# Sixteen tiles of x in a transformer block: for the second eight, 32x32 block turns on VectorE in place of TensorE transposes

## The chip, the cores and the metric

One core of one Trainium2 chip runs the kernel. Its engines are TensorE (PE in the profile), VectorE (DVE), ScalarE (ACT), GpSimd (POOL) and SyncE (SP), which issues most of the DMA transfers. Each engine takes its instructions from a queue of its own, in the order in which they were written, and they meet through semaphores. The metric is the device time of one execution in microseconds, as the median of three runs.

## The reference, cut to what matters

The block works on 2048 rows of 1024 columns in float32.

```
h   = x + attention(layernorm(x))
out = h + relu(layernorm(h) @ w1) @ w2

attention(x): q, k, v = x @ wqkv                 32 heads of 32
              phi_q, phi_k = softmax(+-(q @ w_phi)), softmax(+-(k @ w_phi))
              o = phi_q (phi_k^T v) / (phi_q sum(phi_k) + 1e-6)
              return o @ wo
layernorm(x): (x - mean) / sqrt(var + 1e-5)      per row
```

The layernorm of the first line is the one that the change touches: its output, turned so that the columns of x lie on the partitions, is the stationary operand of the products with the weights of q, k and v.

## The kernel before, in words

The 2048 rows are 16 tiles of 128, in two halves of 8. A float32 product is made of two parts of each operand, a high one (the value rounded to TensorE's fp32r type) and a low one (the value minus the high part), and three matmuls: high by high (L182), high by low of the weight (L183), low by high (L184). So the second of the three needs the weight's low part, and the third needs the low part of x. One such triple is a step, and eight steps (the eight 128-column blocks of x) are an item: one tile by one 128x512 piece of the weights, for each of the 8 blocks k. The first half runs 32 kv items (4 pieces s of the key and value weights by 8 tiles) and 16 q items (2 pieces by 8), and then the second half the same. In steps, the piece of the weights changes at 0, 64, 128, 192 (kv), 256, 320 (q) for the first half and 384, 448, 512, 576 (kv), 640, 704 (q) for the second. This text calls such a place a switch. After these 96 items come the product with wo and the MLP, which the change leaves alone.

Everything beside the matmuls is written into the stream by hand: `when(step, f)` puts the work f behind the matmuls of that step, and so sets its place in the queue of every engine that it uses. What the steps of this text refer to:

- **Weight units** (class Units, L69 to L137). A unit is one 128x512 block of weights: loaded raw, copied to its high part by ACT (L125), and subtracted to its low part by POOL or DVE (L129; in kv pieces the even k go to POOL and the odd ones to DVE). The ring has 10 places and a piece takes 8, so at a switch most units of the next piece are made while PE works on the last item of the old one, each as a place comes free.
- **Layernorm of x** (L211 to L253). A load, the statistics on DVE (`ln_stats`, L222), three instructions on POOL for the scale and shift (`ln_power`, L231 to L233, called the trio here), the normalization on ACT (`ln_norm`, L239), eight PE transposes into two PSUM banks (`ln_turn`, L246), and out of each bank a high part by ACT (L178) and a low part by DVE (L179), into the tile xT.
- **The second half's tiles** (t = 8 to 15). Their statistics and trio are made early, at steps 98+16i and 102+16i (i = t-8). The normalization and the turn come late, around the q items of the last q piece of the first half (steps 320 to 384), where xT of tile t-8 comes free. For that x is loaded a second time.
- **POOL's other work in the same stretch.** `t_sum` (L363) makes sums of blocks of the MLP's weights, in place in a 512 KB tile: a load, four subtractions on POOL, a store (t<-b), with two such tiles, so that a load waits until the store before the last is done. `kv_z` (L452, L454) adds up the key features (zacc). L544 copies small sums of the q items (smq).
- **Places on SP**: SP issues raw loads, t_sum's loads and stores, and the loads of x in program order, and waits in its queue for what each needs.

Of the kernel before, what the change touches and what calls it, by code (L numbers as in the profile page):

```python
# [9 lines left out]
F32 = mybir.dt.float32  # L10
F32R = mybir.dt.float32r
AF = mybir.ActivationFunctionType
ALU = mybir.AluOpType
AX = mybir.AxisListType

P = 128
S = 2048
D = 1024
# [3 lines left out]
NT = S // P  # L22
HT = NT // 2
NK = D // P
# [116 lines left out]
def kernel(  # L141
# [12 lines left out]
    v, act, pool, pe, sp = nc.vector, nc.scalar, nc.gpsimd, nc.tensor, nc.sync  # L154
# [4 lines left out]
    lnp = ctx.enter_context(tc.tile_pool(name="lnp", bufs=2))  # L159
    dram = ctx.enter_context(tc.tile_pool(name="scratch", bufs=1, space=bass.MemoryType.DRAM))  # L160
# [12 lines left out]
    def f32(ap):  # L173
        return ap.bitcast(F32)
# [14 lines left out]
    def do(n, k, f, *args):  # L189
        at[n, k].append((f, args))  # L190
# [6 lines left out]
    ed = [dram.tile([8, 2, P, 512], F32, name=f"ed{b}") for b in range(4)]  # L197
    smd = [dram.tile([2, P, P], F32, name=f"smd{b}") for b in range(4)]
    hd = [dram.tile([P, D], F32, name=f"hd{t}") for t in range(NT)]

# [6 lines left out]
    xin, xst, xnt = {}, {}, {}  # L209

    def ln_load(key, parts):  # L211
        xin[key] = xlp.tile([P, D], F32, name="xl") if key[0] == "x" and key[1] >= HT and key[1] % 4 > 1 else \
            lnp.tile([P, D], F32, name="xin")
        n = D // len(parts)
        for j, p in enumerate(parts):
            sp.dma_start(xin[key][:, j * n:(j + 1) * n], p)
# [10 lines left out]
    def ln_power(key):  # L227

        mv = xst[key]
        sc = scx[:, key[1] - HT, 0, :] if key[0] in "sf" else lnp.tile([P, 2], F32, name="sc", bufs=4)  # L230
        pool.tensor_scalar_add(sc[:, 0:1], mv[:, 1:2], LN_EPS)  # L231
        pool.tensor_tensor(out=sc[:, 0:1], in0=sc[:, 0:1], in1=half, op=ALU.pow)
        pool.tensor_scalar(sc[:, 1:2], mv[:, 0:1], sc[:, 0:1], -1.0, op0=ALU.mult, op1=ALU.mult)  # L233
        xst[key] = sc

    def ln_norm(key):
        sc, src = xst.pop(("s", key[1]) if key[0] == "x" and key[1] >= HT else key), xin.pop(key)
        xnt[key] = src if key[0] == "h" else fp_ln.tile([P, D], F32, name="xn")
        act.activation(xnt[key], src, AF.Identity, bias=sc[:, 1:2], scale=sc[:, 0:1])  # L239

    def ln_turn(key, j, dst=None):
# [10 lines left out]
        if j == 1:  # L252
            del xnt[key]  # L253


    right = ExitStack()
    xpool = right.enter_context(tc.tile_pool(name="xT", bufs=HT, side="right"))
# [2 lines left out]
    fp_ln = kps.enter_context(tc.tile_pool(name="xn", bufs=2, side="right"))  # L260
# [159 lines left out]
    xT = {}  # L420
# [298 lines left out]
    def ln_pair(i, stage):  # L719

        keys = [("h", 4 * r + i) for r in range(2)]
        if stage == 0:
            for key in keys:
                ln_load(key, [hd[key[1]]])
# [222 lines left out]
    def item(gen, *args, keys):  # L947
        items.append((gen, args + (keys,)))
        steps.extend((k,) for k in keys)
        return len(items) - 1  # L950
# [11 lines left out]
    for b, tiles in enumerate(groups):  # L962
        for hf in range(2):

            pairs = b == 0 and hf == 0
            for j in range(0, 4, 2 if pairs else 1):
# [3 lines left out]
                for half in range(2):  # L970
                    n = item(wo_pair, tiles[j:j + 2], hf, half, keys=[("wo", hf, 4 * half + k // 2) for k in range(8)])
# [18 lines left out]
    def x_part(t):  # L990
        return [x[t * P:(t + 1) * P, :]]
# [6 lines left out]
    def when(step, f, *args):  # L998

        if step < 8 * first_up:  # L1000
            do(step // 8, step % 8, f, *args)
        else:
            do(first_up + (step - 8 * first_up) // 4, step % 4, f, *args)
# [4 lines left out]
    for t in range(1, NT):  # L1008
        n = t - 1 if t < HT else q_n[1, t - HT] + 1
        turn = 8 * n + 1  # L1010
        if t < HT:
            stages = X_STEPS.get(t, (turn - 22, turn - 12, turn - 9, turn - 6, turn, turn + 3))
        else:

            early = 80 + 16 * (t - HT)
            when(early, ln_load, ("s", t), x_part(t))
            when(early + 18, ln_stats, ("s", t))
            when(early + 18, xin.pop, ("s", t))
            when(early + 22, ln_power, ("s", t))
            load_ = turn - 88 + 8 * (t - HT) if t < HT + 4 else turn - 36  # L1020
            stages = (load_, None, None, turn - 8, turn + 1, turn + 1)
        for step, f, *args in zip(stages, (ln_load, ln_stats, ln_power, ln_norm), [("x", t)] * 4):
            if step is not None:
                when(step, f, *args, *([x_part(t)] if f is ln_load else []))
        do(n, 0, x_open, t)
        for j in range(2):
            when(stages[4 + j], ln_turn, ("x", t), j, lambda t=t: xT[t])
# [146 lines left out]
    def up_step(b, p, m):  # L1174

        return up0 + 4 * (up_n[b, p, m] + 1 - first_up)

    for j, m in enumerate(UP):

        for g in range(2):  # L1180
            step = up0 + (8 * j + (-62, -29)[g] if j < 4 else 6 * (j - 4) + 4 + 2 * g)
# [4 lines left out]
            step = up_step(0, NP - 1, m) + 2 * j  # L1186
# [16 lines left out]
    for n, (w, p, j) in enumerate((w, p, j) for w in (1, 2) for p in range(NP) for j in range(2)):  # L1203
        step = sums_at[n]
# [7 lines left out]
    for b in range(2):  # L1212
        for m in DOWN:
            n = down_n[b, m, NP - 1] + 1
            name, more = {1: "x1", 5: "x4", 6: "x2", 4: "x3"}.get(m), \
# [15 lines left out]
    scx = consts.tile([P, HT, 4, 2], F32, name="scx")  # L1231
# [18 lines left out]
    ln_stats(("x", 0))  # L1250
    ln_power(("x", 0))
    ln_norm(("x", 0))
    x_open(0)
    ln_load(("x", 2), x_part(2))
# [70 lines left out]
```

## Time and profile before

| | |
|---|---|
| median of 3 runs | 1872.97 us (1872.37 to 1873.45) |
| the profiled execution, its own time | 1870.48 us |
| its span | 1868.7 us |
| PE busy | 1856.5 us, 99% of the span |
| DVE busy | 1063.8 us, 57% |
| POOL busy | 979.0 us, 52% |
| ACT busy | 770.5 us, 41% |
| TensorE clock granted | nine tenths or more in each of 40 slices |
| HBM read, written | 293.21 MB, 137.89 MB |

A row of the timeline has the start in us, the length, the engine, the line of the kernel, the operation with its output and inputs, and in brackets the engine's idle time before it with what ended it. Rows that stand together are a group: xcount is the number of instructions, and the length runs to the end of the last. A matmul's length is that from its entry to its modelled end, and matmuls overlap, so the distance between two starts is the price of one. In the table of groups each row has busy time in all and the mean of one in ns. A row of waits has the total, the number of times and the longest. The names are those of the kernel; L numbers are the lines of the kernel before.

### The profile page before, as it was taken

The numbers are of one execution on the slowest core, as the hardware profiler recorded it, in microseconds if no ns is written. First come the engines' busy times: TensorE is split into PE (matmuls) and PEld (weight loads), VectorE is DVE, ScalarE is ACT, GpSimd is POOL, SyncE is SP. The second block draws the span as 40 slices with busy tenths as digits, with TensorE's granted clock in tenths as the row PEclk, the third lists the DMA queues.
The fourth block names the chain that finished last, engine by engine and source line by source line (L and its number), as shares of the span: only waits on it lengthen the run. The fifth ranks groups of instructions, "written<-read, shape, count | busy, mean of one in ns | idle before, by whom it ended". The sixth has DMA issues, their size and how long they took to land.

```text
span 1868.7 us, 28840 instructions
## 1 busy us (share of the span) xinstructions
PE 1856.5 (99%) x10064; PEld 1516.3 (81%) x10064; DVE 1063.8 (57%) x1655; ACT 770.5 (41%) x1379; POOL 979.0 (52%) x991
## 2 busy tenths in 40 slices
PE   9999999999999999999999999999999999999999
PEld 7777788888887777888888888888888888888887
DVE  7787678677689878575555653443433333343333
ACT  5322245233333333354455554444444444444442
POOL 4887745888947988343333222222344444444443
PEclk9999999999999999999999999999999999999999
DMA  7988798666575676887888975666677677777765
GB/s 229 286 294 288 231 289 270 190 203 202 178 227 181 223 243 203 280 278 232 247 262 259 324 249 184 193 201 205 225 223 215 216 218 239 238 215 217 216 216 177
DMA packets 333635, 433.04 MB, mean 232 GB/s; under 512 B 28720, under 2 KB 194608, under 8 KB 333488
## 3 DMA queue, kind: packets, MB, share of 16 engines
q1 hardware_dynamic: 299696, 414.41, 70.1%
q10 hardware_dynamic: 33792, 16.78, 3.2%
q8 instruction: 79, 1.29, 0.3%
q14 instruction: 68, 0.56, 0.1%
HBM read 293.21 MB, written 137.89 MB: 231 GB/s over the span
## 4 chain that ended last, share of the span: by engine, by line
PE 93%; DVE 3%; POOL 1%; issue 1%; ACT 0%; DMA 0%; SPq 0%; ACTq 0%; DVEq 0%; POOLq 0%
PE mm L182 24%; PE mm L183 24%; PE mm L184 24%; PE ac L182 4%; PE ac L184 4%; PE ac L183 4%; PE tp L184 2%; PE tp L183 2%; PE tp L182 2%; PE tp L246 1%; PE ac L465 1%; PE ac L650 1%; DVE qsm L534 0%; DVE qe L637 0%; POOL w L129 0%
## 5 line engine op out<-in xcount | busy, mean ns | idle before, releaser
L129 POOL TENSOR_TENSOR w<-raw,w 128x512 fp32r<-128x512 f32 x353 | 469.0, 1331 | 698.3 <-ACT w L125 663.2
L125 ACT ACTIVATE w<-raw 128x512 fp32r<-128x512 f32 x686 | 409.4, 626 | 508.8 <-PE mm L184 232.4
L129 DVE TENSOR_TENSOR w<-raw,w 128x512 fp32r<-128x512 f32 x333 | 271.0, 815 | 511.6 <-ACT w L125 507.6
L182 PE MATMUL mm<-w,xT 128*128 128x512 f32 x768 | 306.0, 398 | 0.0
L183 PE MATMUL mm<-w,xT 128*128 128x512 f32 x768 | 300.2, 391 | 0.4 <-POOL w L401 0.4
L184 PE MATMUL mm<-w,xT 128*128 128x512 f32 x768 | 299.6, 390 | 0.0
L182 PE MATMUL mm<-hT,w 128*128 128x512 f32 x672 | 261.5, 389 | 0.0
L183 PE MATMUL mm<-hT,w 128*128 128x512 f32 x672 | 261.5, 389 | 0.0
L184 PE MATMUL mm<-hT,w 128*128 128x512 f32 x672 | 261.5, 389 | 0.0
L182 PEld LDWEIGHTS mm<-w,xT 128*128 128x128 f32 x768 | 144.4, 188 | 35.2 <-issue 4.1
L184 PEld LDWEIGHTS mm<-w,xT 128*128 128x128 f32 x768 | 144.4, 188 | 30.9
L363 POOL TENSOR_TENSOR b<-b 128x256 f32<-128x256 f32 x176 | 143.6, 816 | 48.0 <-DMA b<-in_w_dram 38.6
L183 PEld LDWEIGHTS mm<-w,xT 128*128 128x128 f32 x768 | 144.6, 188 | 29.2 <-POOL w L401 1.0
L184 PE MATMUL mm<-w 128*128 128x512 f32 x392 | 152.6, 389 | 0.0
L182 PE MATMUL mm<-w 128*128 128x512 f32 x392 | 152.6, 389 | 0.0
L183 PE MATMUL mm<-w 128*128 128x512 f32 x392 | 152.6, 389 | 0.0
L182 PEld LDWEIGHTS mm<-hT,w 128*128 128x128 f32 x672 | 126.2, 188 | 26.4
L183 PEld LDWEIGHTS mm<-hT,w 128*128 128x128 f32 x672 | 126.2, 188 | 26.2
L184 PEld LDWEIGHTS mm<-hT,w 128*128 128x128 f32 x672 | 126.2, 188 | 26.0
L183 PEld LDWEIGHTS mm<-w 128*128 128x128 f32 x392 | 73.6, 188 | 15.3
L184 PEld LDWEIGHTS mm<-w 128*128 128x128 f32 x392 | 73.6, 188 | 15.2
L182 PEld LDWEIGHTS mm<-w 128*128 128x128 f32 x392 | 73.6, 188 | 15.3
(173 smaller groups left out, 3106.0 us busy)
## 6 DMA issues: line engine op xcount, KB each, us to landing
raw<-t SPq DMA_DIRECT2D x224, 256.0 KB, 3.9
raw<-ad SPq DMA_DIRECT2D x196, 256.0 KB, 3.0
raw<-in_w_dram SPq DMA_DIRECT2D x168, 256.0 KB, 3.1
ad<-c SPq DMA_DIRECT2D x112, 256.0 KB, 3.6
b<-in_w_dram SPq DMA_DIRECT2D x44, 512.0 KB, 5.8
t<-b SPq DMA_DIRECT2D x44, 512.0 KB, 5.0
ad<-s SPq DMA_DIRECT2D x84, 256.0 KB, 4.1
ed<-qe ACTq DMA_DIRECT2D x64, 256.0 KB, 4.1
```

The costliest lines, as they stand in the source:

```text
L125: nc.scalar.activation(w[:, 0, :], raw[1], AF.Copy)
L129: eng.tensor_tensor(out=w[:, 1, :], in0=raw[1], in1=w[:, 0, :].bitcast(F32), op=ALU.subtract)
L182: pe.matmul(ps, a_hi, b_hi, start=first, stop=False, skip_group_check=more)
L183: pe.matmul(ps, a_hi, b_lo, start=False, stop=False, skip_group_check=more)
L184: pe.matmul(ps, a_lo, b_hi, start=False, stop=last, skip_group_check=more)
L246: pe.transpose(pt[:, k, :], xn[:, (4 * j + k) * P:(4 * j + k + 1) * P], ident)
L363: pool.tensor_tensor(out=tsum[*u, *out], in0=tsum[*u, *a], in1=tsum[*u, *b], op=ALU.subtract)
L465: pe.matmul(kv_ps[s][g][32 * i:32 * (i + 1), 0:64], vt[:, 32 * h:32 * (h + 1)], phi[:, 64 * h:64 * (h + 1)], start=first, stop=last)
L650: pe.matmul(banks[g][32 * c:32 * (c + 1), 256 * j:256 * (j + 1)], kvL[rows, 2 * q + h // 4, 32 * (h % 4):32 * (h % 4 + 1)], phT_of[u - 1 + ...
```

## The change

For the tiles 8 to 15 the late second load, the normalization there, the 64 PE transposes and the reads of PSUM go. In their place:

- **Early**, at steps counted from early = 80+26i: the load at +0, the statistics at +12, the trio at +16, the normalization on ACT at +20 (`far_norm`), which writes the normalized tile into a second buffer with its 32-column blocks exchanged (runs of 128 bytes), and at +23 a store by SP (`far_keep`, 512 KB in pieces of 1 KB) to a DRAM tile xm whose rows and blocks lie so that 32x32 block turns finish the transpose.
- **Late**, at steps counted from late_ = 330+11i: at -30 SP loads the tile back (`far_back`, 512 KB), at +0 DVE turns it in place by 32x32 blocks (`far_turn`, one instruction 128x1024), at +4 ACT makes the high part (`far_high`) and at +7 POOL the low part (`far_low`), one instruction 128x1024 each. Both read the turned tile with an innermost step of 1 KB and write xT in order.

So the low parts of these eight tiles move from DVE (two instructions 128x512 from PSUM) to POOL (one of 128x1024 from SBUF), and the trio moves from steps 102+16i to 96+26i.

```diff
--- before.py
+++ after.py
@@ -197,6 +197,7 @@
     ed = [dram.tile([8, 2, P, 512], F32, name=f"ed{b}") for b in range(4)]
     smd = [dram.tile([2, P, P], F32, name=f"smd{b}") for b in range(4)]
     hd = [dram.tile([P, D], F32, name=f"hd{t}") for t in range(NT)]
+    xm = {t: dram.tile([P, D], F32, name=f"xm{t}") for t in range(HT, NT)}
 
 
 
@@ -209,8 +210,7 @@
     xin, xst, xnt = {}, {}, {}
 
     def ln_load(key, parts):
-        xin[key] = xlp.tile([P, D], F32, name="xl") if key[0] == "x" and key[1] >= HT and key[1] % 4 > 1 else \
-            lnp.tile([P, D], F32, name="xin")
+        xin[key] = lnp.tile([P, D], F32, name="xin")
         n = D // len(parts)
         for j, p in enumerate(parts):
             sp.dma_start(xin[key][:, j * n:(j + 1) * n], p)
@@ -227,14 +227,14 @@
     def ln_power(key):
 
         mv = xst[key]
-        sc = scx[:, key[1] - HT, 0, :] if key[0] in "sf" else lnp.tile([P, 2], F32, name="sc", bufs=4)
+        sc = scx[:, key[1] - HT, 0, :] if key[0] == "f" else lnp.tile([P, 2], F32, name="sc", bufs=4)
         pool.tensor_scalar_add(sc[:, 0:1], mv[:, 1:2], LN_EPS)
         pool.tensor_tensor(out=sc[:, 0:1], in0=sc[:, 0:1], in1=half, op=ALU.pow)
         pool.tensor_scalar(sc[:, 1:2], mv[:, 0:1], sc[:, 0:1], -1.0, op0=ALU.mult, op1=ALU.mult)
         xst[key] = sc
 
     def ln_norm(key):
-        sc, src = xst.pop(("s", key[1]) if key[0] == "x" and key[1] >= HT else key), xin.pop(key)
+        sc, src = xst.pop(key), xin.pop(key)
         xnt[key] = src if key[0] == "h" else fp_ln.tile([P, D], F32, name="xn")
         act.activation(xnt[key], src, AF.Identity, bias=sc[:, 1:2], scale=sc[:, 0:1])
 
@@ -252,6 +252,33 @@
         if j == 1:
             del xnt[key]
 
+
+    def far_norm(t):
+        sc, src = xst.pop(("s", t)), xin.pop(("s", t))
+        xin["m", t] = y = lnp.tile([P, D], F32, name="xin")
+        act.activation(y.rearrange("p (a c k) -> p c a k", a=4, c=NK), src.rearrange("p (c a k) -> p c a k", a=4, c=NK),
+                       AF.Identity, bias=sc[:, 1:2], scale=sc[:, 0:1])
+
+    def far_keep(t):
+        sp.dma_start(xm[t].rearrange("(a t) (g x) -> (t g) a x", a=4, g=4),
+                     xin.pop(("m", t)).rearrange("p (a x) -> p a x", a=4))
+
+    def far_back(t):
+        xnt["x", t] = y = xlp.tile([P, D], F32, name="xl") if t % 4 > 1 else fp_ln.tile([P, D], F32, name="xn")
+        sp.dma_start(y, xm[t])
+
+    def far_turn(t):
+        v.transpose(xnt["x", t], xnt["x", t])
+
+    def far_view(y):
+        return y.rearrange("p (g c t) -> p c t g", g=4, c=NK)
+
+    def far_high(t):
+        act.activation(xT[t][:, 0].rearrange("p c (t g) -> p c t g", g=4), far_view(xnt["x", t]), AF.Copy)
+
+    def far_low(t):
+        lo, hi = (xT[t][:, s].rearrange("p c (t g) -> p c t g", g=4) for s in (1, 0))
+        pool.tensor_tensor(out=lo, in0=far_view(xnt.pop(("x", t))), in1=f32(hi), op=ALU.subtract)
 
     right = ExitStack()
     xpool = right.enter_context(tc.tile_pool(name="xT", bufs=HT, side="right"))
@@ -1012,13 +1039,17 @@
             stages = X_STEPS.get(t, (turn - 22, turn - 12, turn - 9, turn - 6, turn, turn + 3))
         else:
 
-            early = 80 + 16 * (t - HT)
+            early, late_ = 80 + 26 * (t - HT), 330 + 11 * (t - HT)
             when(early, ln_load, ("s", t), x_part(t))
-            when(early + 18, ln_stats, ("s", t))
-            when(early + 18, xin.pop, ("s", t))
-            when(early + 22, ln_power, ("s", t))
-            load_ = turn - 88 + 8 * (t - HT) if t < HT + 4 else turn - 36
-            stages = (load_, None, None, turn - 8, turn + 1, turn + 1)
+            when(early + 12, ln_stats, ("s", t))
+            when(early + 16, ln_power, ("s", t))
+            when(early + 20, far_norm, t)
+            when(early + 23, far_keep, t)
+            when(late_ - 30, far_back, t)
+            do(n, 0, x_open, t)
+            for step, f in ((0, far_turn), (4, far_high), (7, far_low)):
+                when(late_ + step, f, t)
+            continue
         for step, f, *args in zip(stages, (ln_load, ln_stats, ln_power, ln_norm), [("x", t)] * 4):
             if step is not None:
                 when(step, f, *args, *([x_part(t)] if f is ln_load else []))
```

On PE the only difference in order is that the eight rows of L246 between triples of the second half's tiles are gone. On POOL two places matter. The first is the switch of step 128: `w<-raw,w` are low parts of the weight units for that switch, `b<-b` is t_sum, and the trio is L231 to L233. Before:

```order
L231 TENSOR_SCALAR scx<-mv 128x1
L232 TENSOR_TENSOR scx<-scx,half 128x1
L233 TENSOR_SCALAR scx<-mv,scx 128x1
L363 TENSOR_TENSOR b<-b 128x256 x2
L129 TENSOR_TENSOR w<-raw,w 128x512
L363 TENSOR_TENSOR b<-b 128x256
L454 TENSOR_TENSOR zacc_361<-zacc_361,kphi 128x512
L363 TENSOR_TENSOR b<-b 128x256
L129 TENSOR_TENSOR w<-raw,w 128x512 x2
```

The kernel with the change, the same place:

```order
L390 TENSOR_TENSOR b<-b 128x256 x2
L129 TENSOR_TENSOR w<-raw,w 128x512
L390 TENSOR_TENSOR b<-b 128x256
L231 TENSOR_SCALAR sc<-mv 128x1
L232 TENSOR_TENSOR sc<-sc,half 128x1
L233 TENSOR_SCALAR sc<-mv,sc 128x1
L481 TENSOR_TENSOR zacc_369<-zacc_369,kphi 128x512
L390 TENSOR_TENSOR b<-b 128x256
L129 TENSOR_TENSOR w<-raw,w 128x512 x2
```

The trio that stood ahead of the batch now stands in it, in front of the addition to zacc and of the last two weight units. The second place on POOL is the stretch from the switch of step 384 (its last unit opens the rows) towards that of step 448. Before:

```order
L129 TENSOR_TENSOR w<-raw,w 128x512
L363 TENSOR_TENSOR b<-b 128x256
L544 TENSOR_TENSOR smq<-qsm 128x16 x2
L363 TENSOR_TENSOR b<-b 128x256 x3
L454 TENSOR_TENSOR zacc_360<-zacc_360,kphi 128x512
L544 TENSOR_TENSOR smq<-qsm 128x16 x2
L363 TENSOR_TENSOR b<-b 128x256 x4
L454 TENSOR_TENSOR zacc_360<-zacc_360,kphi 128x512
L363 TENSOR_TENSOR xn<-xn 128x256 x4
L454 TENSOR_TENSOR zacc_360<-zacc_360,kphi 128x512
L363 TENSOR_TENSOR xn<-xn 128x256 x4
```

With the change, where L281 is `far_low`, L390 is t_sum, L481 is kv_z and L571 is the copy of small sums:

```order
L129 TENSOR_TENSOR w<-raw,w 128x512
L281 TENSOR_TENSOR xT<-xn,xT 128x1024
L390 TENSOR_TENSOR b<-b 128x256
L571 TENSOR_TENSOR smq<-qsm 128x16 x2
L390 TENSOR_TENSOR b<-b 128x256 x3
L481 TENSOR_TENSOR zacc_368<-zacc_368,kphi 128x512
L281 TENSOR_TENSOR xT<-xl,xT 128x1024
L571 TENSOR_TENSOR smq<-qsm 128x16 x2
L390 TENSOR_TENSOR b<-b 128x256 x4
L481 TENSOR_TENSOR zacc_368<-zacc_368,kphi 128x512
L390 TENSOR_TENSOR xn<-xn 128x256 x2
L281 TENSOR_TENSOR xT<-xl,xT 128x1024
```

Three instructions of 128x1024 now stand among the same work, the low parts of tiles 13, 14 and 15; that of tile 12 stands just ahead of these rows, before two copies of small sums. The four subtractions of one t_sum tile (xn) now stand on both sides of the last low part.

## The prediction

> **What bounds the kernel now.** I read the head of the profile first, then PE's waits, then the timelines of PE and POOL around the switches. From the head, and the first rows of PE's waits:
>
> ```profile
> span 1868.7 us, 28840 instructions
> PE 1856.5 (99%) x10064; PEld 1516.3 (81%) x10064; DVE 1063.8 (57%) x1655; ACT 770.5 (41%) x1379; POOL 979.0 (52%) x991
> ```
>
> ```profile
> PE ac L650 <- DVE qe L637: 2.8, 2, 2.4
> PE tp L246 <- ACT xn L239: 2.2, 1, 2.2
> PE tp L1244 <- POOL ones L1240: 1.6, 1, 1.6
> PE mm L183 <- POOL wf L129: 1.5, 1, 1.5
> PE mm L183 <- POOL w L401: 0.4, 1, 0.4
> ```
>
> PE bounds it: 1856.5 of 1868.7 us, and its waits sum to 8.5 us. None is longer than 2.4 us. So the change can gain only what leaves PE's queue, and loses whatever new wait it puts in front of a matmul. The other engines are half idle on average, which says nothing of the places where PE is close behind them.
>
> **What it removes from PE.** The timeline of PE around the turn of one tile of the second half:
>
> ```profile
> 268.10 0.39 PE L184 MATMUL mm<-w,xT 128*128 128x512 f32 x1
> ...
> 268.78 0.39 PE L184 MATMUL mm<-w,xT 128*128 128x512 f32 x1
> 269.01 1.03 PE L246 MATMUL tp<-ident,xn 128*128 128x128 f32 x8
> ...
> 270.35 0.39 PE L184 MATMUL mm<-w,xT 128*128 128x512 f32 x1
> ```
>
> From one L184 to the next a step takes 268.78 - 268.10 = 0.68 us; with the eight transposes between, 270.35 - 268.78 = 1.57. A tile's transposes cost 0.89 us of PE, though the row says 1.03 (overlap). Eight tiles: 8 x 0.89 = 7.15 us. They start behind a matmul, without idle time, so all of it is gained if nothing else is late. PE then reaches the switch of step 384 seven tiles, 6.26 us, earlier, and all later work 7.15 us earlier.
>
> **What it puts on the other engines.** The nearest groups:
>
> ```profile
> L239 ACT ACTIVATE xn<-xin,scx 128x1024 f32<-128x1024 f32 x4 | 5.0, 1241 | 4.5 <-DMA xl<-in_x_dram 2.1 <-DMA raw<-in_wv_dram 1.4 <-ACT qe L525 1.0
> L178 ACT ACTIVATE xT<-tp 128x512 fp32r<-128x512 f32 x32 | 17.9, 595 | 20.5 <-PE tp L246 20.4
> L179 DVE TENSOR_TENSOR xT<-tp,xT 128x512 fp32r<-128x512 f32 x32 | 20.7, 679 | 11.1 <-ACT xT L178 11.1
> L637 DVE STREAM_TRANSPOSE qe<-qe 128x1024 f32<-128x1024 f32 x32 | 39.3, 1227 | 7.5 <-POOL qe L631 5.6 <-POOL qe L626 1.8
> L781 DVE STREAM_TRANSPOSE y<-xin 128x1024 f32<-128x1024 f32 x4 | 8.2, 2040 | 1.2 <-ACT xin L796 1.2
> L579 POOL TENSOR_TENSOR xl<-xl,zb 128x1024 f32<-128x1024 f32 x6 | 14.4, 2401 | 0.0
> t<-b SPq DMA_DIRECT2D x44, 512.0 KB, 5.0
> ```
>
> - DVE, per tile: one in-place turn, 1.23 us by L637, for two subtractions of 0.68. That is neutral, -0.13 us.
> - ACT, per tile: the normalization stays (1.24 us by L239), and one copy of 128x1024 takes the place of two of 0.60. Bounds for the copy: 1.2 (no price for the strided read) to 2.0 (1.2 x 2040/1227, the ratio of L781, which writes in 16-byte steps, to L637, which doesn't). I take 1.6: +0.4 us on an engine 41% busy. I cost it at nothing: the moved normalizations stand ahead of no weight unit that they could delay by more than their own 1.24 us, and ACT has idle time before each unit.
> - SP and DMA: eight loads of 512 KB go and eight come; eight stores of 512 KB are new. The like of them, t<-b, lands in 5.0 us; the steps between store and reading back are over 100 for every tile, and 30 steps (30 x 0.68 = 20 us) lie between load and turn. A store waits in SP's queue for ACT's normalization, and raw loads stand behind it; they are issued some 20 us before use. Cost nothing, bounds -1 to +2 us.
> - POOL: +8 low parts of 128x1024, and the trios moved. This is what decides.
>
> **The trios, early.** The timeline of POOL around the switch of step 128, and PE's use of the last unit but one that POOL makes there:
>
> ```profile
> 109.41 0.22 POOL L231 TENSOR_SCALAR scx<-mv 128x1 f32<-128x1 f32 x1 [2.91 <-DVE mv L224]
> ...
> 110.38 0.70 POOL L233 TENSOR_SCALAR scx<-mv,scx 128x1 f32<-128x1 f32 x1
> ...
> 115.34 1.77 POOL L454 TENSOR_TENSOR zacc<-zacc,kphi 128x512 f32<-128x512 f32 x1
> 117.08 1.18 POOL L363 TENSOR_TENSOR b<-b 128x256 f32<-128x256 f32 x1
> 118.22 3.00 POOL L129 TENSOR_TENSOR w<-raw,w 128x512 fp32r<-128x512 f32 x2
> ```
>
> ```profile
> 120.75 0.39 PE L183 MATMUL mm<-w,xT 128*128 128x512 f32 x1
> ```
>
> The trio takes 109.41 to 111.08, 1.67 us, in a gap of POOL. With the change it stands ahead of the row of 115.34, behind which POOL has no gap until the two units are done, the first at 118.22 + 1.50 = 119.72. PE takes that one at 120.75, so there is 1.03 us of room; 1.67 - 1.03 = 0.64 is the most it can be late. I take 0.5. The trio of tile 14 (step 252) stands in the same way inside the batch for step 256; I give it 0.3, between nothing and 0.64. The other six fall between switches. Sum 0.8 us, bounds 0 and 1.3.
>
> **The low parts, late.** POOL, and PE's first use of a POOL unit after the switch of step 384:
>
> ```profile
> 275.35 3.19 POOL L363 TENSOR_TENSOR b<-b 128x256 f32<-128x256 f32 x4 [5.12 <-DMA b<-in_w_dram]
> 282.12 3.20 POOL L363 TENSOR_TENSOR b<-b 128x256 f32<-128x256 f32 x4 [3.23 <-DMA b<-in_w_dram]
> 289.08 2.39 POOL L363 TENSOR_TENSOR b<-b 128x256 f32<-128x256 f32 x3 [3.41 <-DMA b<-in_w_dram]
> 296.14 0.74 POOL L363 TENSOR_TENSOR b<-b 128x256 f32<-128x256 f32 x1 [3.62 <-DMA b<-in_w_dram]
> 302.76 3.19 POOL L363 TENSOR_TENSOR b<-b 128x256 f32<-128x256 f32 x4 [2.85 <-DMA b<-in_w_dram]
> 306.71 1.28 POOL L129 TENSOR_TENSOR w<-raw,w 128x512 fp32r<-128x512 f32 x1 [0.77 <-ACT w L125]
> ```
>
> ```profile
> 312.99 0.39 PE L183 MATMUL mm<-w,xT 128*128 128x512 f32 x1
> ```
>
> Before step 384 POOL runs at the pace of t_sum's transfers, a sum every 6.9 us whatever PE does, and its last sum ends at 302.76 + 3.19 = 305.95. PE, 6.26 us earlier, wants the first unit at 312.99 - 6.26 = 306.73; POOL can have it at 305.95 + 1.28 = 307.23 at best. That is 0.5 us late, and I take 0.8 for the queue behind it (bounds 0 and 1.5). This is a wait that the gain itself makes. The low parts of tiles 8 to 11 fall into the gaps of 3.23, 3.41, 3.62 and 2.85 us behind the sums: up to about 3.2 us each they are hidden but for 0.4 in the last, and above that the sums slip.
>
> The low parts of tiles 12 to 15 fall into the stretch behind it. One row of the table of busy time by stretch for all of 312.7 to 348, and the first unit of the next switch, step 448:
>
> ```profile
> 312.70:348.00 35.30, 35.30 (x204) 29.05 (x204) 25.72 (x52) 8.65 (x16) 27.05 (x35) 1.00 0.85 255
> ```
>
> ```profile
> 353.12 1.30 POOL L129 TENSOR_TENSOR w<-raw,w 128x512 fp32r<-128x512 f32 x1 [5.12 <-ACT w L125]
> ```
>
> POOL is busy for 27.05 us of it (the last column of busy times). With the change that work starts at about 310.2 (307.2, and 3 us for the two units and the copies ahead), so it ends at 310.2 + 27.05 + 4L = 337.25 + 4L, where L is the price of one low part. It must be over when ACT hands over the first unit of step 448: 353.12 - 7.15 + 0.8 = 346.8, and 0.8 us of room behind that (as at the other switches, where it was 1.03 above), 347.6. At L = 2.4 the end is 346.85, no wait; above, each 0.1 us of L costs 0.4 us.
>
> **The price L.** No row shows a GpSimd subtraction that reads with a 1 KB step. Low end: 2.40 us, L579, two streams of 128x1024. High end: 2.40 x 2040/1227 = 4.0, the whole instruction dearer by the ratio that strided access costs a DVE turn. Only one of its two input streams is strided, so I take half of 2.40 as dearer by that ratio: 2.40 + 1.20 x 0.66 = 3.2.
>
> [...]
>
> **The sum.** With L = 3.2: 7.15 - 0.8 (trios) - 0.8 (step 384) - 0.4 (last gap) - 2.8 (337.25 + 12.8 - 347.6 = 2.45, and 0.35 for POOL's waits among it) = 2.35 us. Against the profiled execution's 1870.48 that gives 1868.1; its time stood 2.5 us under the median of 1872.97, and the forecast for the median is 1872.97 - 2.35 = 1870.6, say 1870.7. By the price of both bounds the gain lies between 7.15 - 1.6 = 5.5 (L = 2.4) and about -3.3 (L = 4.0: sums slip by 4 x 0.72 = 2.9, the stretch costs 6.0).
>
> **The rivals.**
> - Strided reads cost POOL nothing: L = 2.4, all low parts hidden, gain 5.5, 1867.5. For it: GpSimd's contiguous rows (2.40 us for 1024 columns) are far slower than a DVE row, so the access may not be its limit. Against: L781.
> - The other side: POOL becomes the bound around the switches of steps 384 and 448, since the whole instruction pays. It decides from the L at which the gain is eaten: 7.15 - 1.6 - (4 x (L - 3.28)) - (4 x (L - 2.4) - 0.4) = 0 at L = 3.6. At 4.0, and 0.3 more for subtractions of DVE beside it, L = 4.3: 4 x 1.02 + 7.2 = 11.3 against 5.55, slower by 5.7, 1878.7.
> - L = 3.6, midway between 3.2 and 4.0, as if one stream and part of the other paid: the gain is just eaten, 1873. [...]
> - All eight moved trios stand in PE's way, not two: 8 x 0.64 = 5.1 in place of 0.8, 1870.7 + 4.3 = 1875. Against: six stand between switches, where POOL's units have microseconds to spare.
> - The change doesn't do what it says, the transposes' time returning as idle time before other matmuls: excluded up to the waits named, since PE waits so little today.
>
> **How the numbers follow.** Chances: L near 3.2 0.33 (its own range 1868.5 to 1873), L near 2.4 0.25, L near 3.6 0.12, L from 4.0 0.23, all trios 0.07. The time forecast is that of the first. No measurement of this kernel tells less than about 0.2%, 3.75 us, from no change. Faster by more, below 1869.2, takes L under 2.9: all of the second case and a sixth of the first, 0.30. Slower by more, above 1876.7, takes L over 4.0: most of the fourth, half of the fifth and a quarter of the third, 0.28. Within it 0.42. The range reaches from 1866.5, under the second case, to 1879.5, over the fourth.
>
> **What would show it.** PE: no L246 with 128x128 x8 after the first tiles, and steps of 0.68 us where 1.57 stood. POOL: the mean of the new low part is L; 2.4, 3.2, 3.6 and 4.3 tell the cases apart. PE's waits: new rows "L183 <- POOL w L129" (at its new line), a few tenths at 120 and 222 us, under 1 at about 306 and some 2.5 at 346; nothing after 350. DVE's turn at 1.23, ACT's copy between 1.2 and 2.0. Wrong would be a wait of PE for DVE or for ACT, for low parts of x themselves (L184), or for a raw load held up behind a store.

## The result, and the profile after

The changed kernel is slower: 1880.29 us median (1879.02 to 1882.84, 6 runs) against 1872.38 (1872.02 to 1873.45), a ratio of 1.0041 (95% interval 1.0031 to 1.0052). The profiled execution took 1881.46 us, 10.98 more than the one of before.

The page's head and the waits of PE in the changed kernel (total, times, longest):

```profile
span 1879.7 us, 28708 instructions
PE 1856.4 (99%) x10000; PEld 1512.1 (80%) x10000; DVE 1071.4 (57%) x1647; ACT 778.0 (41%) x1371; POOL 1002.4 (53%) x999
```

```profile
PE mm L183 <- POOL w L129: 5.4, 5, 3.4
PE ac L492 <- DVE kphi L473: 3.6, 1, 3.6
PE ac L677 <- DVE qe L664: 2.9, 2, 2.4
PE tp L246 <- ACT xn L239: 2.2, 1, 2.2
...
PE mm L183 <- DVE w L129: 1.0, 1, 1.0
PE mm L182 <- ACT w L125: 0.5, 1, 0.5
```

PE's busy time is the same to 0.1 us, though 64 transposes have gone: the matmuls took longer in some places. The waits have grown from 8.4 to 19.3 us. The groups that stand for the moved work:

```profile
L281 POOL TENSOR_TENSOR xT<-xn,xT 128x1024 fp32r<-128x1024 f32 x4 | 11.8, 2958 | 0.0
L277 ACT ACTIVATE xT<-xl 128x1024 fp32r<-128x1024 f32 x4 | 8.4, 2098 | 17.2 <-DVE xl L271 13.1 <-DMA b<-in_w_dram 4.1
L271 DVE STREAM_TRANSPOSE xl<-xl 128x1024 f32<-128x1024 f32 x4 | 4.9, 1222 | 0.0
```

So L is 2.92 to 2.96 us in the mean of four, here taken as 2.95, under the 3.2 of the forecast. The places of the loss come out when the start of the same step is compared in both traces. Worked out from the PE timelines, the changed kernel's lag behind the one before, in us (a turn that PE no longer does lowers it by 0.9):

| step | 0 | 112 | 144 | 256 | 272 | 320 | 336 | 384 | 400 | 416 | 432 | 448 | 464 | 760 |
|---|---|---|---|---|---|---|---|---|---|---|---|---|---|---|
| lag | 0.57 | 0.63 | 1.23 | 1.30 | 1.81 | 1.81 | 2.11 | -3.35 | 2.45 | 2.45 | 7.83 | 7.83 | 9.35 | 9.37 |

The six turns between 336 and 384 save 5.46 us, as forecast. Behind step 384 the lag grows by 5.8 us, and since the eighth turn lies there too, 6.7 are lost; behind step 416 another 5.4, behind 448 another 1.5. The PE timeline has these three, with the idle time in brackets:

```profile
313.96 0.79 PE L183 MATMUL mm<-w,xT 128*128 128x512 f32 x1 [3.36 <-POOL w L129]
314.55 0.63 PE L184 MATMUL mm<-w,xT 128*128 128x512 f32 x1
314.98 0.63 PE L182 MATMUL mm<-w,xT 128*128 128x512 f32 x1
```

```profile
345.66 0.43 PE L492 MATMUL ac<-kphi,vt 128*32 128x64 f32 x16 [3.62 <-DVE kphi L473]
```

```profile
370.16 0.50 PE L183 MATMUL mm<-w,xT 128*128 128x512 f32 x1 [1.23 <-POOL w L129]
```

Behind 314 us a matmul takes 0.63 us and the next starts 0.43 later, where 0.39 and 0.23 are usual. The table of stretches shows why, for 6 us behind the first wait, 4.3 behind the second and 4.8 behind the third (the last three numbers of a row are the granted clock, the DMA share and GB/s):

```profile
314.00:320.00 6.00, 6.00 (x17) 4.73 (x18) 5.89 (x8) 1.75 (x4) 6.00 (x5) 0.60 0.83 232
345.70:350.00 4.30, 4.30 (x26) 3.36 (x27) 3.47 (x9) 1.01 (x2) 4.30 (x3) 0.60 0.69 168
370.20:375.00 4.80, 4.80 (x21) 3.99 (x22) 3.29 (x6) 1.00 (x3) 4.80 (x4) 1.00 0.73 239
```

The 0.60 is a mean: in finer stretches the clock is 0.50 from 312.1 to 318.8 us and 1.00 from 318.9, and again 0.50 from 346.2 to 349.5 and 1.00 from 349.6. So these two waits, of 3.36 and 3.62 us, cost their length, and then matmuls run for 4.8 and 3.3 us at half the clock: behind step 384, 6.7 us are lost for 3.9 of waits, behind 416, 5.4 for 3.6. That is part of why PE's busy time has not fallen; where the rest of it lies stays open.

What made GpSimd late at 314 us is its sum loop. The five sums of t_sum before step 384, in the changed kernel's POOL timeline, the first and the last with the unit behind it:

```profile
280.51 3.20 POOL L390 TENSOR_TENSOR b<-b 128x256 f32<-128x256 f32 x4 [4.89 <-DMA b<-in_w_dram]
...
309.04 3.63 POOL L390 TENSOR_TENSOR b<-b 128x256 f32<-128x256 f32 x4 [0.56 <-DMA b<-in_w_dram]
312.63 2.96 POOL L129 TENSOR_TENSOR w<-raw,w 128x512 fp32r<-128x512 f32 x2
```

They ran from 275.35 to 305.95 before. Already the first is 5.2 us late, and the loop, which runs at the latency of its transfers (its sums begin 7.1 us apart in the mean, 6.9 before), never makes it up: the last is 6.3 us late. The loads of tiles 12 and 13 into the xn buffers, which stand in SP's queue ahead of a t_sum load each, wait for the low parts of tiles 8 and 9 on GpSimd; the waits of SP from 285 to 350 us have it:

```profile
SPq L268 <- POOL xT L281: 5.1, 2, 2.7
```

That did not slow the loop. The two loads went out at 286.67 and 293.44 us, and the t_sum loads behind them at 288.84 and 296.40, each as soon as an earlier store of the loop had landed, at 288.77 and 296.39.

### The profile page after: what moved, and what is told of

It reads as the page before. It is cut to its first block, busy times and chain, and to the rows that moved or that the text cites. A ratio compares the mean times of both kernels' runs of the same rounds, so it can differ in the third digit from the quotient of the medians.

```text
span 1879.7 us, 28708 instructions
## 1 busy us (share of the span) xinstructions
PE 1856.4 (99%) x10000; PEld 1512.1 (80%) x10000; DVE 1071.4 (57%) x1647; ACT 778.0 (41%) x1371; POOL 1002.4 (53%) x999
## 4 chain that ended last, share of the span: by engine, by line
PE 86%; POOL 4%; DMA 4%; DVE 4%; issue 1%; ACT 0%; SPq 0%; ACTq 0%; POOLq 0%; DVEq 0%
PE mm L182 22%; PE mm L183 22%; PE mm L184 21%; PE ac L182 4%; PE ac L183 4%; PE ac L184 4%; PE tp L183 2%; PE tp L184 2%; PE tp L182 2%; DMA b<-in_w_dram 2%; POOL b L390 1%; POOL w L129 1%; DMA raw<-in_wv_dram 1%; DMA t<-b 1%; PE ac L492 1%
## 5 line engine op out<-in xcount | busy, mean ns | idle before, releaser
L129 DVE TENSOR_TENSOR w<-raw,w 128x512 fp32r<-128x512 f32 x333 | 276.8, 832 | 515.4 <-ACT w L125 510.0
L390 POOL TENSOR_TENSOR b<-b 128x256 f32<-128x256 f32 x176 | 144.3, 820 | 36.1 <-DMA b<-in_w_dram 25.5
L481 POOL TENSOR_TENSOR zacc<-zacc,kphi 128x512 f32<-128x512 f32 x60 | 81.6, 1360 | 11.4 <-DVE kphi L473 11.4
L182 PEld LDWEIGHTS mm<-w 128*128 128x128 f32 x392 | 73.6, 188 | 15.3
L183 PEld LDWEIGHTS mm<-w 128*128 128x128 f32 x392 | 73.6, 188 | 15.2
```

Of the source, the lines that this page charges most:

```text
L129: eng.tensor_tensor(out=w[:, 1, :], in0=raw[1], in1=w[:, 0, :].bitcast(F32), op=ALU.subtract)
L182: pe.matmul(ps, a_hi, b_hi, start=first, stop=False, skip_group_check=more)
L183: pe.matmul(ps, a_hi, b_lo, start=False, stop=False, skip_group_check=more)
L390: pool.tensor_tensor(out=tsum[*u, *out], in0=tsum[*u, *a], in1=tsum[*u, *b], op=ALU.subtract)
L481: pool.tensor_tensor(out=zacc[s], in0=zacc[s], in1=phi_of[key], op=ALU.add)
```

## The experiments

Lags below are those of the profiled executions, read as in the table above. Small differences at step 0 (up to 2.8 us in one trace) are of the start and stand in all later columns; so each column is the growth of the lag over 16 steps (384 to 400, 416 to 432, 448 to 464).

| run | median us | ratio, 95% interval | lag grown behind 384 | behind 416 | behind 448 |
|---|---|---|---|---|---|
| changed kernel | 1880.29 | 1.0041 (1.0031 to 1.0052) | 5.8 | 5.4 | 1.5 |
| low parts on VectorE | 1881.05 | 1.0051 (1.0036 to 1.0066) | 5.5 | 6.7 | 0.0 |
| fifth sum moved | 1877.06 | 1.0025 (1.0016 to 1.0034) | 0.6 | 7.0 | 0.2 |
| early stage moved | 1875.56 | 1.0018 (1.0009 to 1.0028) | 0.6 | 5.7 | 1.5 |
| both moved | 1873.05 | 1.0003 (0.9994 to 1.0013) | -0.9 | 4.6 | 1.6 |
| both, low parts cut | 1875.26 | 1.0016 (1.0007 to 1.0026) | 0.1 | 1.4 | 6.6 |
| both, kv_third later | 1875.56 | 1.0016 (1.0006 to 1.0025) | 1.0 | 0.0 | 8.8 |
| both, late stage closer | 1872.91 | 1.0002 (0.9992 to 1.0011) | 7.1 | 0.0 | 0.0 |
| room, kv_third as it was | 1875.02 | 1.0014 (1.0005 to 1.0023) | -0.5 | 7.4 | 0.0 |
| room, kv_third later | 1869.97 | 0.9990 (0.9981 to 0.9999) | -0.3 | 1.9 | 0.0 |
| room, later, two low parts cut | 1869.45 | 0.9980 (0.9971 to 0.9989) | 1.4 | 0.0 | 1.0 |

The eighth turn lies behind step 384: -0.9 there is that turn alone, no wait, and what is lost there is 0.9 more than the entry, 6.7 us in the changed kernel. The run with the low parts read straight through has 4.9, 5.5 and 0.9, in a single execution.

**The low parts on VectorE.**

```diff
-        pool.tensor_tensor(out=lo, in0=far_view(xnt.pop(("x", t))), in1=f32(hi), op=ALU.subtract)
+        v.tensor_tensor(out=lo, in0=far_view(xnt.pop(("x", t))), in1=f32(hi), op=ALU.subtract)
```

> The low parts of tiles 8 to 15 on VectorE in place of GpSimd, nothing else changed. Theory Q (the low parts on GpSimd are what makes its units late at step 384): PE's waits of 3.4 us near 314 us and of 3.6 us near 346 us both go, about 1869 us. Theory S (the five t_sum tiles of steps 332 to 372 run at the latency of their transfers and end after PE needs the units of step 384, with or without the low parts): the wait near 314 us shrinks to 1 to 2.5 us and does not go, 1873 to 1877 us. Theory D (VectorE is itself too full there: 1.4 to 2 us more a tile): a new wait for kphi of 2 us or more, 1875 us or above.

It measured 1881.05 us; a subtraction took 2.1 us (tiles with xl) or 2.5 us (xn) in the mean. Its PE waits at step 384 are shorter and come of VectorE too, and the wait for kphi is longer:

```profile
313.65 0.80 PE L183 MATMUL mm<-w,xT 128*128 128x512 f32 x1 [1.88 <-DVE w L129]
...
346.68 0.65 PE L492 MATMUL ac<-kphi,vt 128*32 128x64 f32 x16 [5.03 <-DVE kphi L473]
```

So theory D holds: VectorE has no room for them. Theory Q falls: without low parts on GpSimd the five sums still ran from 278.73 to 309.39 us. Two of them were stretched here from 3.2 to 4.7 us, beside VectorE's low parts.

**The fifth sum moved.**

```diff
-        [266, 276, 286, 296, 332, 342, 352, 362, 372] + [64 * i + k for i in (6, 7, 8, 9) for k in sixth] + [650]
+        [266, 276, 286, 296, 332, 342, 352, 362] + [64 * i + k for i in (6, 7, 8, 9) for k in sixth] + [643, 654]
```

> The fifth t_sum tile of the q stretch (step 372) is taken out and done after step 640 instead; low parts stay on GpSimd. Theory S: GpSimd's last sum before step 384 ends about 7 us earlier, the wait near 314 us goes, and the wait for kphi near 346 us goes with it, as it follows from raw loads and units that came late after the first: 1880.3 - 5.8 - 5.4 = 1869 us. Rival C (the second wait has a cause of its own: GpSimd's low parts hold VectorE, ScalarE stands behind the turn): only the first goes, 1874 to 1875 us. Theory Q: the low parts still make it late, at most 2 us gained, 1878 us or above.

The growth behind 384 fell from 5.8 to 0.6 us, as theory S had it. The wait for kphi stayed (3.99 us, 7.0 lost), so rival C holds for that one. The time, 1877.06, is 2 us above what C gave; the second loss came out 1.6 us larger.

**The early stage moved.**

```diff
-            early, late_ = 80 + 26 * (t - HT), 330 + 11 * (t - HT)
+            early, late_ = (80, 102, 124, 146, 182, 204, 226, 248)[t - HT], 330 + 11 * (t - HT)
```

> The early stage of tiles 8 to 15 at steps 80, 102, 124, 146, 182, 204, 226, 248, so that none of the trios falls on a switch; the rest as in the changed kernel. If the trios make the waits of 0.30 us at 122 us and 0.19 us at 224 us, these two go and about 1.1 us is gained, 1879 us. If the stores and normalizations of the early stage make them, they stay and the time with them, 1880 us.

The waits at 122 and 224 us are gone, and with them the 1.1 us that was expected. The surprise is that the growth behind 384 fell to 0.6 us as well, with all five sums in place: the first began at 274.39 us and the last ended at 305.81. So the half of theory S that has the sums end too late in any case is wrong: they are late because they start late.

How the early stage made them start late shows in the changed kernel's trace. The trio of tile 15 (step 278) stands on GpSimd between the subtractions of a t_sum tile:

```profile
240.37 1.55 POOL L390 TENSOR_TENSOR b<-b 128x256 f32<-128x256 f32 x2 [3.97 <-DMA b<-in_w_dram]
242.01 0.22 POOL L231 TENSOR_SCALAR sc<-mv 128x1 f32<-128x1 f32 x1
```

VectorE had the statistics for it at 234.87 us, but it came behind the load of that sum. ScalarE's normalization waited for the trio, and the exponential of a q item behind it, whose input was there at 238.8 us, ran at 244.43. The timelines of ScalarE and VectorE:

```profile
243.28 1.24 ACT L259 ACTIVATE xin<-xin,sc 128x1024 f32<-128x1024 f32 x1 [8.82 <-POOL sc L233]
...
261.80 3.24 ACT L125 ACTIVATE w<-raw 128x512 fp32r<-128x512 f32 x6 [1.00 <-PE mm L184]
```

```profile
258.42 0.69 DVE L547 TENSOR_TENSOR qe<-mm,qmx 128x512 f32<-128x512 f32 x1 [1.79 <-DMA ed<-qe]
```

In between stand two stores. That of tile 15 went out at 245.41 and took 6.7 us to land; a store of q features in ScalarE's queue went out only then, at 252.13 (by the trace's semaphores it waited for the first), and landed at 258.30. VectorE waited for it, the next exponential ran at 259.74, and behind that the six high parts of weight units. In the kernel before they began 4.0 us earlier, while PE was only 1.8 us ahead of the changed kernel:

```profile
257.84 3.24 ACT L125 ACTIVATE w<-raw 128x512 fp32r<-128x512 f32 x6 [1.16 <-PE mm L184]
```

The raw loads, and behind them on SP the load of the first sum (272.14 for 268.59 us), followed. In all four runs with the early stage of the changed kernel ScalarE stood idle for 8.8 to 9.5 us before that normalization, and the first sum began at 278.7 to 280.5 us; in the five with the early stage moved and no sum put at step 306 the idle time was at most 3.5 us and the first sum began at 274.4 to 277.1. No run moved the stage of tile 15 alone.

**A low part read straight through.**

```diff
-        pool.tensor_tensor(out=lo, in0=far_view(xnt.pop(("x", t))), in1=f32(hi), op=ALU.subtract)
+        pool.tensor_tensor(out=xT[t][:, 1], in0=xnt.pop(("x", t)).rearrange("p (c k) -> p c k", c=NK),
+                           in1=f32(xT[t][:, 0]), op=ALU.subtract)
```

> The low part of tiles 8 to 15 reads the turned tile straight through in place of with a 1 KB step, so the low parts hold values of other places; all else is the same. If the step of the reading makes the price, the instruction of 128x1024 falls from 2.95 us to the 2.40 us of the other two-stream rows; if the write in the rounded type or the neighbours on VectorE make it, it stays at 2.9 us. Time: 0 to 4 us less than 1880.

The group of the low part in that run:

```profile
L281 POOL TENSOR_TENSOR xT<-xn,xT 128x1024 fp32r<-128x1024 f32 x4 | 9.6, 2405 | 0.0
```

2.40 us, so the 1 KB step makes the price: 0.55 us on top, 1.23 times. The time was 1880.51 us in a single run, and PE still waited 3.36 us at 314 and 3.75 for kphi: the price of the low part isn't what lost the time.

**Both moved.** The two edits together.

> Both edits of before together: the trios off the switches, the fifth t_sum tile after step 640. If the wait for kphi near 340 us has a cause of its own, it stays at 3.5 to 4 us with some 6 us of loss, everything else of the new waits is gone: 1871 to 1873 us. If it follows from GpSimd's lateness at step 384, it is under 1 us: 1866 to 1867 us.

All new waits up to step 384 are gone, the one for kphi stays (2.79 us), and 1.23 us at step 448: 1873.05, even with the kernel before. A cause of the wait for kphi shows on VectorE and GpSimd of this run, by their timelines:

```profile
318.96 3.19 DVE L129 TENSOR_TENSOR w<-raw,w 128x512 fp32r<-128x512 f32 x1
...
329.38 1.79 DVE L473 TENSOR_TENSOR kphi<-ke,ksm 128x512 f32<-128x512 f32 x1
...
336.01 1.02 DVE L473 TENSOR_TENSOR kphi<-ke,ksm 128x512 f32<-128x512 f32 x1
```

```profile
318.65 2.95 POOL L281 TENSOR_TENSOR xT<-xn,xT 128x1024 fp32r<-128x1024 f32 x1
327.68 2.95 POOL L281 TENSOR_TENSOR xT<-xl,xT 128x1024 fp32r<-128x1024 f32 x1
```

A subtraction that takes 0.64 to 0.68 us alone takes 3.19 and ends 0.55 us after the low part beside it. The kphi that PE waits for is the third, which ends at 336.01 + 1.02 = 337.03 us. In the kernel before, whose VectorE timeline has it so, it ended at 333.13, 3.9 us earlier, though PE came later there:

```profile
332.44 0.69 DVE L446 TENSOR_TENSOR kphi<-ke,ksm 128x512 f32<-128x512 f32 x1
```

**The low parts cut in four.** For all eight tiles:

```diff
-        pool.tensor_tensor(out=lo, in0=far_view(xnt.pop(("x", t))), in1=f32(hi), op=ALU.subtract)
+        src = far_view(xnt.pop(("x", t)))
+        for c in range(0, NK, 2):
+            pool.tensor_tensor(out=lo[:, c:c + 2], in0=src[:, c:c + 2], in1=f32(hi)[:, c:c + 2], op=ALU.subtract)
```

> As the run with both edits, and each low part of tiles 8 to 15 on GpSimd cut into four instructions of 128x256. Theory K (a VectorE instruction with two inputs in SBUF stands still while a GpSimd instruction runs, to that instruction's end): the 3.19 us of VectorE's weight subtraction beside a low part and the 1.79 us of kphi fall to 1.5 us or less, the wait for kphi falls from 4.0 to 1.5 us or less, and the time by 3 to 4 us. Rival H (ScalarE's high part stands ahead of the exponential and waits for the turn): VectorE's durations may fall, the wait stays above 3 us and the time within 1 us.

The same places:

```profile
319.43 1.11 DVE L129 TENSOR_TENSOR w<-raw,w 128x512 fp32r<-128x512 f32 x1
...
328.29 1.00 DVE L475 TENSOR_TENSOR kphi<-ke,ksm 128x512 f32<-128x512 f32 x1
...
334.15 0.78 DVE L475 TENSOR_TENSOR kphi<-ke,ksm 128x512 f32<-128x512 f32 x1
```

What theory K says of the two engines agrees with the traces: VectorE's weight subtraction, both inputs in SBUF, ended 0.55 us behind the whole low part; beside the four pieces, which run from 319.12 to 322.95 us, 0.96 us each in the mean, it takes 1.11 us for 3.19 and ends at 320.54, about 0.46 behind the first piece, not behind a tile's work. Subtractions with one input in PSUM weren't held: in the changed kernel two of them, at 285.27 and 285.87 us, took 0.67 each beside the low part of 283.66 to 286.63. The third kphi now ends at 334.93 us, 2.1 of the 3.9 us earlier, and the wait for it fell from 2.79 to 1.21 us, so rival H isn't the whole cause. The other 1.8 us aren't separated: two turns of 1.2 us stand ahead of the third kphi on VectorE, and ScalarE's high parts, which wait for them, ahead of its exponentials. The time didn't fall as theory K forecast, but rose by 2.2 us: PE, now earlier, waited 3.37 and 1.35 us for GpSimd's units at step 448, and four pieces take 3.83 us of GpSimd for 2.95.

**kv_third later.**

```diff
-        when(8 * (n + (2, 1, 0, 2, 1, 0, 1, 0)[t % HT]) + 22, kv_third, (hf, s, t))
+        when(8 * (n + (2, 1, 0, 2, 1, 0, 1, 0)[t % HT]) + (28 if (hf, s) == (1, 0) and t % HT < 3 else 22), kv_third, (hf, s, t))
```

> As the run with both edits, and the first group of kv_third of the second half (tiles 8 to 10, first piece) asked for six steps (4.1 us) later on PE. If the wait for kphi is one late group and the engines have caught up behind it, it goes, and 5.4 to 6.5 us are gained: about 1866.5 us. If VectorE and ScalarE stay late, the next group waits in its place for 2 us or more and less than 3 us is gained.

Both readings missed: the wait for kphi went entirely and no later group took it over, but GpSimd's units at step 448 did, with 4.17 and 1.75 us, and 8.8 us were lost there; 1875.56 us. What GpSimd has to do between the switches of 384 and 448 doesn't fit into PE's time for it; the wait for kphi had only hidden that.

**The late stage closer.**

```diff
-            late_ = 330 + 11 * (t - HT)
+            late_ = 330 + 8 * (t - HT)
...
-            when(late_ - 30, far_back, t)
+            when(late_ - 20, far_back, t)
```

> As the run with both edits, and the late stage of tiles 8 to 15 at steps 330+8i in place of 330+11i (load 20 steps ahead), so that it ends at step 393, before the kv items of the second half have begun in earnest. If the turns, high parts and low parts beside the first kv items make the wait for kphi, it falls under 1 us; the eight low parts then stand among the four t_sum tiles, and a wait of 0 to 2.5 us for GpSimd's units comes back near 310 us: 1867 to 1871 us. If not, kphi still waits 3 us or more.

The waits went as expected, though dearer: none for kphi and none at step 448, and at 384 waits of 0.92 (for ScalarE), 0.85, 3.35 and 0.37 us (for GpSimd), by which the lag grew by 7.1 us. The time, 1872.91 us, is above the forecast. The load of four low parts is pushed from one switch to the other.

**Room on GpSimd.** On top of the early stage moved, the fifth sum of the q stretch goes to step 306 and two of the six sums between 384 and 448 behind step 640:

```diff
-        [266, 276, 286, 296, 332, 342, 352, 362, 372] + [64 * i + k for i in (6, 7, 8, 9) for k in sixth] + [650]
+        [266, 276, 286, 296, 306, 332, 342, 352, 362] + [394, 409, 424, 439] + \
+        [64 * i + k for i in (7, 8, 9) for k in sixth] + [640, 647, 654]
```

With kv_third later:

> As the run with trios off the switches, and room made on GpSimd: the fifth t_sum tile of the q stretch goes ahead of it (step 306), two of the six t_sum tiles between the switches of steps 384 and 448 go behind step 640, and the first group of kv_third of the second half is asked for six steps later. If what GpSimd has to do between steps 384 and 448 is the bound (four low parts of 2.95 us came in, 11.8 us, and 6.4 us go out here), the waits near 310, 337 and 360 us are all under 1 us and most of the 7.15 us is kept: 1866 to 1868 us. If GpSimd isn't the bound there, a wait of 3 us or more comes back: 1872 us or above.

and with kv_third as it was:

> The same with kv_third where it was. If the wait for kphi comes of VectorE being held by the low parts (durations 3.2 and 1.8 us as before), it stays at 2.5 to 4 us: 1870 to 1873 us, 4 to 5.5 us above the run with kv_third later. If it came of GpSimd's load alone, it goes and the two are the same.

With kv_third later only two of the new waits are left in that part of the PE timeline, 1.72 us for kphi and 0.32 for a unit:

```profile
310.24 0.50 PE L183 MATMUL mm<-w,xT 128*128 128x512 f32 x1 [0.32 <-POOL w L129]
339.12 0.43 PE L492 MATMUL ac<-kphi,vt 128*32 128x64 f32 x16 [1.72 <-DVE kphi L473]
```

1869.97 us, 0.1% under the kernel before (the interval ends at 0.9999), though 2 us short of the forecast. Behind step 448 nothing is lost any more, so what GpSimd had to do was the bound there. With kv_third where it was the wait for kphi is 5.70 us, though GpSimd has two sums less to do, so it doesn't come of GpSimd's load; 1875.02, 5 us above. It is longer than before since, with fewer sums ahead of it, a low part starts just before the very kphi that PE waits for, which its timelines of VectorE and GpSimd show:

```profile
336.64 3.08 DVE L473 TENSOR_TENSOR kphi<-ke,ksm 128x512 f32<-128x512 f32 x1
```

```profile
336.32 2.85 POOL L281 TENSOR_TENSOR xT<-xl,xT 128x1024 fp32r<-128x1024 f32 x1
```

**Two low parts cut.** On top of that, with kv_third later, only the low parts of tiles 13 and 14 in four pieces.

> As the run with room made on GpSimd and kv_third later, and the low parts of tiles 13 and 14, the two that ran beside VectorE's weight subtraction and kphi, cut into four instructions each. Theory K: VectorE's 3.2 us there falls to 1.1 us as it did in the cut run before, the wait of 1.7 us for kphi near 339 us goes or falls under 0.4 us, and 1.5 to 2 us are gained: about 1868.3 us. Against it: the cut parts cost GpSimd 0.9 us more each, and a wait for its units near 360 us takes the place: 1870 us or above.

VectorE's subtraction beside the low part of tile 13 takes 1.14 us. The wait for kphi is gone; waits of 0.17, 0.41 and 0.84 us near 310 and 0.66 at 357 us came in its place. 1869.45 us, ratio 0.998 (0.9971 to 0.9989): the best version, 0.5 us under the run without the cuts, which these runs can't tell apart.

**Waits of known length in the kernel before.** Between two transposes on PE, ScalarE copies ident onto itself n times:

```diff
+    def stall(n):
+        pe.transpose(tp_bank()[:, 0:P], ident, ident)
+        for _ in range(n):
+            act.activation(ident, ident, AF.Copy)
+        pe.transpose(tp_bank()[:, 0:P], ident, ident)
+    for step, n in ((420, 3), (484, 8), (548, 14), (612, 21)):
+        when(step, stall, n)
```

> The kernel before, with PE held up at four steps between switches (420, 484, 548, 612) by a chain of 3, 8, 14 and 21 small copies on ScalarE between two transposes: waits of about 0.8, 2.1, 3.6 and 5.4 us. If a long wait costs more than its length because the clock granted behind it falls (theory G), the two long ones cost 1.3 to 1.6 us beyond their length and show a clock of 0.6 to 0.8 in the 5 us behind, the short one nothing: 1872.5 + 12 + 3 to 5 = 1887.5 to 1889.5 us. If the low clock in the changed kernel had another cause, such as its DMA load, each costs its length: 1884.5 us.

The copies were dearer than thought, so the waits were longer: 1.08, 2.79, 4.83 and 7.22 us. The lag grew by 1.54, 4.65, 6.79 and 9.79 us. Taking 0.46 us off each for the two transposes and the pipeline (what the first cost beyond its wait, with the clock at 1.00 behind it), the others cost 1.4, 1.5 and 2.1 us more than their length. The stretches of 5 us behind each:

```profile
339.10:344.10 5.00, 5.00 (x66) 3.93 (x67) 1.15 (x4) 0.38 (x1) 4.69 (x7) 1.00 0.81 249
390.00:395.00 5.00, 5.00 (x60) 3.68 (x61) 0.00 (x0) 1.01 (x5) 4.08 (x7) 0.69 0.38 126
444.30:449.30 5.00, 5.00 (x60) 3.71 (x61) 0.00 (x0) 0.90 (x5) 3.37 (x6) 0.66 0.14 47
501.00:506.00 5.00, 5.00 (x57) 3.75 (x58) 0.00 (x0) 0.82 (x4) 3.37 (x6) 0.52 0.00 0
```

Theory G holds. The DMA share behind the long waits is 0.38, 0.14 and 0.00, and the clock is low all the same. 1894.12 us, 21.5 above before, for 15.9 us of waits; that is above the forecast, which had 12 us of them.

## Why the prediction was wrong

It forecast 1870.7 us, and by its sum a slower time would need a low part of 3.6 us or more. The low part was 2.95 us, and the kernel is slower all the same. In the profiled execution 7.15 us left PE and 18.1 us came in: 6.7 behind step 384, 5.4 behind 416, 1.5 behind 448, 1.1 for two trios and 3.4 elsewhere.

- **What leaves PE** was right: 0.89 us a tile forecast, 5.46 for six measured.
- **The prices** were near: turn 1.22 us (1.23 forecast), ScalarE's high part 2.1 (1.6 taken, above the upper bound of 2.0), low part 2.95 (3.2 taken). The 3.2 was the author's estimate, 1.33 times the 2.40, with half of it dearer by the ratio of two turns on VectorE; the runs show 1.23 times, 2.40 without the step and 2.95 with it.
- **The early stage, the step that failed first.** The trios at steps 128 and 256 cost 0.6 and 0.5 us, for 0.5 and 0.3. But "The other six fall between switches" took it that an early stage costs nothing there, and the normalizations were said to delay no weight unit "by more than their own 1.24 us". Tile 15's held ScalarE for 8.82 us, as its trio came late on GpSimd behind a sum, and six high parts of weight units came 4.0 us late, the first sum 5.2.
- **Step 384** is where that is paid. 0.8 us stood there and 0.4 for the last gap, with a sum loop at its own pace "whatever PE does"; 6.7 were lost. The loop keeps its pace and also keeps every delay. The gaps of 2.9 to 3.6 us were counted as room for the low parts, and hid them about as said; they weren't room for a late start. With the early stage moved 1.5 us were lost, the upper bound of the 0.8.
- **The wait for kphi wasn't in the sum at all.** "I cost it at nothing" was said of ScalarE, and VectorE's turn was balanced against two subtractions. Left out were two things: the late stages of tiles 13 to 15 stand beside the first kv items, and VectorE's subtractions and kphi with both inputs in SBUF ended only behind a low part of 2.95 us that ran beside them (3.18 us for 0.68 and 1.77 for 0.69 in the changed kernel, each 0.55 us behind the low part's end). It lost 5.4 us, of which the runs show the second as a cause and not as the only one. A wait of PE for DVE was among the signs of being wrong that the prediction named.
- **Step 448** cost 1.5 us. That the stretch's formula gives as much at L = 2.95 (337.25 + 11.8 - 347.6 = 1.45) is luck: it counts on a PE 6.35 us ahead of the kernel before, and in the run PE was 7.8 us behind it there. In the run without the wait for kphi the loss is 8.8 us. So the rival "POOL becomes the bound around the switches of steps 384 and 448" had the right place, with a condition that was wrong: L need not be 3.6 or more, 11.8 us of added work, at 2.95 each, is enough.
- **The clock** was left out: in the run with built waits, 2.79 us and more cost 1.4 to 2.1 us beyond their length. Of the three waits that decided, two were that long.
- **The rest**: 1.6 us more between step 760 and the end (a wait of 1.03 us for VectorE at 619 us among it), 1.2 us between steps 320 and 336 and 0.6 at the start; no run was made for these. Between store and reading back lie 92 steps for tile 15, not over 100; nothing came of that.

## What to carry to other kernels

When PE is 99% busy and one engine is taken off its queue, look at what the other engines are paced by: a loop through DRAM that ends in time today can keep a delay that is put ahead of it (here 5.2 us at its first sum and 6.3 at its last), and work that fits between two weight switches by its sum may not fit when PE comes sooner. Short work put between two sums of such a loop comes as late as the loop, and holds whatever stands behind it in the next queue (here ScalarE, for 8.82 us). A low part of 2.95 us on GpSimd was also a price on VectorE's subtractions with two inputs in SBUF beside it, 3.19 us for 0.68; cutting it in four lowered that to 1.11, but cost GpSimd 3.83 us for 2.95. And removing one wait shows the next one: a gain, of 0.1 to 0.2%, came only when sums, early stage and the consumer's place were moved together.

## What the runs showed of the hardware

A built wait of PE of 1.08 us left the granted clock at 1.00 over the 5 us behind it; one of 2.79 us was followed by 0.69, one of 4.83 by 0.66, and one of 7.22 us by 0.52, with matmuls 0.43 us apart in place of 0.23. In finer stretches the clock is 0.50 and then 1.00: in the changed kernel 0.50 from 312.1 to 318.8 and from 346.2 to 349.5 us, and in the kernel before, behind a wait of 2.38 us, from 591.94 to 595.03. The length alone doesn't decide: in the run with kv_third later, behind a wait of 2.74 us that ended at 596.01, the matmuls stood 0.23 us apart.

A GpSimd subtraction of 128x1024 took 2.40 us read straight through and 2.95 with one input at a 1 KB step; ScalarE's copy of the same shape took 1.05 us read straight through (the copies of hT, L863 of the changed kernel) and 2.1 with that step.
